# Rotating the last sums through two PSUM banks, and moving transposes and sums within their slots

## The chip, the cores and the metric

One core of a Trainium2 chip. The metric is the time of one execution in device microseconds (us), lower is better. PE is TensorE, PEld its weight loads, DVE is VectorE, ACT is ScalarE, POOL is GpSimd, SP is SyncE, which here issues nearly all transfers. PSUM is the memory that PE writes its sums to, and a bank is one block of it.

## The reference

A retention layer (a recurrence with decay per head) feeds a mixing layer. Shapes: batch 4, 8 heads, sequence 768, head size 64, so 512 channels.

```python
for t in range(S):
    state = gamma * state + einsum('bhd,bhe->bhde', k[:, :, t], v[:, :, t])
    x[:, :, t] = scale * einsum('bhd,bhde->bhe', q[:, :, t], state)
# x as (batch, seq, 512)
theta = x @ w_theta
zr, zi = x * cos(theta), x * sin(theta)
y = w_tok_r @ zr + w_tok_i @ zi          # along the sequence
u = x + y
out = u + relu(u @ w_ch)
```

## The kernel before

The sequence of each batch is cut into three groups of 256 rows, so there are twelve groups n = 0 to 11 for the first half (flip k and q, the masked products, theta, z), and 24 tiles m = 0 to 23 of 128 rows for the second. A loop slot n works on group n, finishes group n - 1, and carries one tile of the second half in slots 3 to 6 and two in slots 7 to 12. The order of the program is the order on each engine.

One tile of the second half is 12 products into y, an addition on DVE that gives u, a transpose of u, four products o, and an output on DVE:

```python
def moe_M(m, lo, hi):                     # y sum, 2 products for each of 6 s0
    b, t0 = divmod(m, nT)
    if lo == 0:
        mo[m] = dict(y=psum.tile([P, dm], FT, name="y_ps", tag="y", bufs=1))
    y_ps = mo[m]["y"]
    ...
def moe_u(m):
    ...
    nc.vector.tensor_add(u, mo[m]["y"], xs[b][:, t0, :])
```

PE may not start the next tile's sum in a bank before DVE has read the last one out of it. The end of the kernel, tiles 18 to 22:

```python
for m in range(last_m - nT + 1, last_m):
    moe_U_dma(m - 1)                      # transpose of u by DMA
    moe_M(m, 0, 4)
    ...
    moe_O(m - 2); moe_out(m - 2); store(m - 2)
    moe_M(m, 4, nT)
    moe_u(m)
moe_last(last_m)
```

The place before the loop:

```python
moe_M(0, 5, nT)
prep(3, "q", DP)        # q scaled, half on DVE, half on POOL
moe_u(0)
prep(3, "v", PP)        # on POOL
w_cast(3)               # on POOL
moe_M(1, 0, 4)          # overwrites the y bank: waits for u of tile 0
flip(3, "q")
moe_M(1, 4, nT)
moe_u(1)
```

The first loop slot, n = 3, puts on POOL: the scaling of q and v of group 4, the casts of w row 4, the cast of wch (the weights of o).

## Time and profile before

| | kernel before |
|---|---|
| median before the prediction | 180.67 us, three runs, 179.34 to 180.89 |
| the profiled run | 179.78 us, span 178.1, mean granted clock 0.998 |
| busy, share of the span | PE 90%, PEld 50%, DVE 57%, ACT 46%, POOL 36% |
| chain that ended last | PE 78%, DMA 6%, DVE 5%, ACT 4%, issue 3%, POOL 3% |

PE is what ends last, so the other engines matter only where PE waits for them.

### The profile page before, as it was taken

How to read it: one execution, taken by the hardware profiler on the slowest of the kernel's cores; microseconds unless marked ns; L12 is line 12 of the kernel's file. 1: busy time of each engine (PE TensorE's matmuls, PEld its weight loads, DVE VectorE, ACT ScalarE, POOL GpSimd, SP SyncE). 2: the span in 40 equal slices, each digit the busy share in tenths (PEclk: the TensorE clock that was granted, in tenths of full speed). 3: DMA queues.
4: the chain of work that ended last, by engine and by line, in shares of the span. 5: the costliest groups of instructions: out<-in, count | busy, mean ns of one | idle time of the engine just before them, and what ended most of it. 6: DMA issues, size and time to landing. Idle time of an engine off the chain costs nothing.

```text
span 178.1 us, 4704 instructions
## 1 busy us (share of the span) xinstructions
PE 161.1 (90%) x1979; PEld 89.5 (50%) x1979; DVE 102.4 (57%) x139; ACT 82.6 (46%) x141; POOL 63.5 (36%) x81
## 2 busy tenths in 40 slices
PE   7889898959889999989999999999999898888892
PEld 2455565624646757555654655545555343333371
DVE  2266698795726777777572983827646154333333
ACT  7236494832456768585738727183471700000000
POOL 5284656490999675914544370000000000000000
PEclk9999999999999999999999999999999999999999
DMA  5999999999999999599999977949163524533343
GB/s 147 312 327 330 288 301 337 339 349 281 337 272 308 291 333 307 137 219 284 223 302 211 292 117 175 162 95 193 30 184 55 156 51 147 95 94 93 94 128 121
DMA packets 66789, 37.92 MB, mean 213 GB/s; under 512 B 24144, under 2 KB 61264, under 8 KB 66768
## 3 DMA queue, kind: packets, MB, share of 16 engines
q1 hardware_dynamic: 66624, 37.50, 82.4%
q8 instruction: 15, 0.25, 0.6%
q10 hardware_dynamic: 144, 0.13, 0.2%
q14 instruction: 6, 0.05, 0.1%
HBM read 25.69 MB, written 6.29 MB: 180 GB/s over the span
## 4 chain that ended last, share of the span: by engine, by line
PE 78%; DMA 6%; DVE 5%; ACT 4%; issue 3%; POOL 3%; DVEq 0%; POOLq 0%
PE y_ps L324 32%; PE o_ps L352 11%; PE th_ps L302 11%; DMA pair<-in_q_dram 6%; PE at_ps L204 4%; PE yT_ps L227 3%; PE y_ps L443 3%; PE kq_ps L183 3%; PE yT_ps L241 3%; PE st_ps L258 3%; DVE u L331 2%; POOL kqb L175 2%; PE y_ps L398 2%; DVE at L211 1%; PE w_ps L378 1%
## 5 line engine op out<-in xcount | busy, mean ns | idle before, releaser
L324 PE MATMUL y_ps<-z,wtr 128*128 128x512 bf16 x138 | 52.4, 379 | 6.2 <-DVE u L331 5.8
L324 PE MATMUL y_ps<-z,wti 128*128 128x512 bf16 x138 | 52.3, 379 | 0.0
L331 DVE TENSOR_TENSOR u<-y_ps,x_sb 128x512 bf16<-128x512 f32 x23 | 15.9, 691 | 32.8 <-PE y_ps L324 32.8
L175 POOL TENSOR_TENSOR kqb<-pair,qscp 128x512 bf16<-128x512 f32 x20 | 22.1, 1123 | 34.8 <-DMA pair<-in_q_dram 32.7
L211 DVE TENSOR_TENSOR at<-at_ps,maskp 128x1024 bf16<-128x1024 f32 x24 | 29.2, 1219 | 2.8 <-PE at_ps L204 2.8
L281 ACT CAST xT<-yT_ps 128x512 bf16<-128x512 f32 x22 | 15.0, 739 | 28.3 <-PE yT_ps L227 28.3
L175 POOL TENSOR_TENSOR kqb<-pair,vscp 128x512 bf16<-128x512 f32 x24 | 25.6, 1085 | 3.0 <-DMA pair<-in_v_dram 2.6
L359 DVE SCALAR_TENSOR_TENSOR ot<-o_ps,u 128x512 f32<-128x512 f32 x23 | 15.9, 690 | 16.5 <-PE o_ps L352 16.3
L324 PEld LDWEIGHTS <-wti 128*128 128x128 bf16 x138 | 13.5, 98 | 20.8 <-issue 8.0
L302 PE MATMUL th_ps<-wth,xT 128*128 128x512 bf16 x96 | 23.5, 379 | 0.1
L352 PE MATMUL o_ps<-wch,uT 128*128 128x512 bf16 x92 | 22.6, 379 | 0.0
L324 PEld LDWEIGHTS <-wtr 128*128 128x128 bf16 x138 | 13.4, 97 | 14.2
L305 ACT ACTIVATE cs<-th_ps,halfpi 128x512 bf16<-128x512 f32 x24 | 16.5, 689 | 8.3 <-PE th_ps L302 7.9
L272 ACT CAST stbd<-st_ps 64x256 bf16<-64x256 f32 x40 | 14.7, 367 | 10.8 <-PE st_ps L258 10.2
L312 DVE TENSOR_TENSOR z<-cs,x_sb 128x1024 bf16<-128x1024 bf16 x24 | 19.0, 829 | 0.0
L186 DVE COPY kqT<-kq_ps 128x1024 bf16<-128x1024 bf16 x17 | 11.5, 687 | 12.0 <-PE kq_ps L183 11.9
L306 ACT ACTIVATE cs<-th_ps,zerob 128x512 bf16<-128x512 f32 x24 | 16.5, 688 | 0.0
L169 ACT CAST kqb<-pair 128x1024 bf16<-128x1024 f32 x12 | 12.6, 1048 | 6.8 <-DMA pair<-in_k_dram 6.8
L410 ACT COPY uT<-u_ps 128x256 bf16<-128x256 bf16 x2 | 0.7, 372 | 31.2 <-PE u_ps L409 31.2
L352 PEld LDWEIGHTS <-uT 128*128 128x128 bf16 x92 | 9.0, 98 | 10.4
L302 PEld LDWEIGHTS <-xT 128*128 128x128 bf16 x96 | 8.9, 98 | 9.9 <-ACT xT L281 0.6
L443 PE MATMUL y_ps<-warm 128*128 128x512 bf16 x31 | 10.9, 478 | 1.3 <-DVE warm L115 1.3
(57 smaller groups left out, 162.8 us busy)
## 6 DMA issues: line engine op xcount, KB each, us to landing
pair<-in_k_dram SPq DMA_DIRECT2D x12, 512.0 KB, 6.8
pair<-in_q_dram SPq DMA_DIRECT2D x12, 512.0 KB, 7.8
pair<-in_v_dram SPq DMA_DIRECT2D x12, 512.0 KB, 8.3
out_dram<-ot SPq DMA_DIRECT2D x23, 256.0 KB, 2.3
wtok<-in_moe_w_tok_r_dram SPq DMA_DIRECT2D x6, 384.0 KB, 6.9
wtok<-in_moe_w_tok_i_dram SPq DMA_DIRECT2D x6, 384.0 KB, 6.4
w<-in_moe_w_theta_dram SPq DMA_DIRECT2D x1, 1024.0 KB, 8.0
w<-in_moe_w_ch_dram SPq DMA_DIRECT2D x1, 1024.0 KB, 9.1
```

The costliest lines, as they stand in the source:

```text
L175: engines[two].tensor_mul(dst[:, two], src[:, two], _bcast_last(sc[:, 2 * g + two], D))
L211: nc.vector.tensor_mul(at.rearrange("p a j t -> p (a j) t"), at_ps.rearrange("p a j t -> p (a j) t"), _bcast_mid(maskp[:, two].rearrange(" ...
L281: copy(st[n, "xT"][:, a].rearrange("e j (i w) -> e j w i", w=2), st[n, "y"][a].rearrange("e j (w i) -> e j w i", w=2))
L302: nc.tensor.matmul(th_ps, st[n, "xT"][:, a, j, :], wth[:, j, :], start=(j == 0), stop=(j == NP - 1))
L305: nc.scalar.activation(cs[:, 0, :], th_ps, AF.Sin, bias=halfpi, scale=1.0)
L306: nc.scalar.activation(cs[:, 1, :], th_ps, AF.Sin, bias=zerob, scale=1.0)
L312: nc.vector.tensor_mul(zs[b][:, c], st[n, "cs", a], _bcast_mid(xs[b][:, c, :], 2))
L324: nc.tensor.matmul(y_ps, wT[r][:, s0, t0 * P:(t0 + 1) * P], zs[b][:, s0, r, :], start=(s0 == 0 and r == 0), stop=(s0 == nT - 1 and r == 1))
L331: nc.vector.tensor_add(u, mo[m]["y"], xs[b][:, t0, :])
L352: nc.tensor.matmul(o_ps, mo[m]["uT"][:, j, :], wch[:, j, :], start=(j == 0), stop=(j == nD - 1))
L359: nc.vector.scalar_tensor_tensor(ot, mo[m]["o"], 0.0, mo[m]["u"], ALU.max, ALU.add)
L443: nc.tensor.matmul(warm_ps, warm[:, 0:P], warm, start=True, stop=True)
```

## The change

Its intent: let the sums of the last tiles alternate between two banks, so that PE need not wait for DVE between tiles; and put work that PE can already do into the holes of the early slots. No work is added or removed.

```diff
     def moe_M(m, lo, hi):
         if lo == 0:
-            mo[m] = dict(y=psum.tile([P, dm], FT, name="y_ps", tag="y", bufs=1))
+            if m < (B - 1) * nT - 1:
+                y_ps = psum.tile([P, dm], FT, name="y_ps", tag="y", bufs=1)
+            else:
+                y_ps = psum.tile([P, dm], FT, name="y_ps", tag="acc", bufs=2)
+            mo[m] = dict(y=y_ps)
 ...
     moe_M(0, 5, nT)
+    moe_u(0)
     prep(3, "q", DP)
-    moe_u(0)
 ...
     moe_u(1)
+    w_tok(3)
     prep(4, "k", K)
 ...  (in the loop)
-        if n == nG:
-            w_tok(3)
 ...
+        if not two and n + 1 >= K_DMA:
+            moe_M(first, 2, 4)
 ...
+        if not two:
+            if n + 1 < K_DMA:
+                moe_M(first, 2, 4)
+            if n in (nG, nG + 1):
+                w_tok(n - nG + 4)
+            moe_M(first, 4, nT)
+            moe_u(first)
+        elif n in pairs:
             moe_M(mine[1], 0, nT)
 ...
         for t in done:
             moe_O(t)
             moe_out(t)
+        if n not in pairs:
+            moe_M(mine[1], 0, nT)
+            moe_u(mine[1])
```

In this code `first` is the slot's first tile (`mine[0]` in the old code), `two` is true in slots with two tiles, nG is 3, `pairs` are the twelve groups (so `n not in pairs` means slot 12), and K_DMA is 7, the first group whose k is flipped by a transfer and not by PE. Smaller lines of the diff (renames, lines that only move) are cut at the marks.

So there are four parts: the end (banks, and the order of slot 12), u of tile 0 ahead of q's scaling, the transposes of w row 3 one slot earlier, and the split of the y sums in slots 3 to 6.

More of the change, by code (lines that the diff above doesn't have):

```diff
@@ L595 @@
             load(n + 3, "q")
-        part = 3 if two else 2
-        moe_M(mine[0], 0, part)
+        first = mine[0]
+        moe_M(first, 0, 3 if two else 2)
         if late:
@@ L603 @@
         if two:
-            moe_M(mine[0], part, nT)
-            moe_u(mine[0])
-        if n == nG:
-            w_tok(3)
-        for name, first in (("k", K_DMA), ("q", Q_DMA)):
-            if nxt and n + 1 < first:
+            moe_M(first, 3, nT)
+            moe_u(first)
+        for name, limit in (("k", K_DMA), ("q", Q_DMA)):
+            if nxt and n + 1 < limit:
                 flip(n + 1, name)
+        if not two and n + 1 >= K_DMA:
+            moe_M(first, 2, 4)
         if nxt and n + 1 >= Q_DMA:
@@ L617 @@
         if n + 1 >= U_DMA:
-            moe_U_dma(mine[0])
+            moe_U_dma(first)
         if n in pairs:
@@ L628 @@
             moe_U(done)
-        if n in (nG, nG + 1):
-            w_tok(n - nG + 4)
-        if two:
+        if not two:
[4 more added lines that the diff above has]
+            moe_M(first, 4, nT)
+            moe_u(first)
+        elif n in pairs:
             moe_M(mine[1], 0, nT)
-        else:
-            moe_M(mine[0], part, nT)
-            moe_u(mine[0])
         if n + 2 in pairs:
@@ L640 @@
             zmul(n - 1, 1)
-        if two:
+        if two and n in pairs:
             moe_u(mine[1])
```

## The prediction

> **What bounds the kernel now.** I read the page first: the span is 178.1 us, TensorE (PE) is busy 90% of it at a granted clock of 0.9 or more throughout, and the chain that ended last is PE work for 78%. So only time in which PE stands still can be gained, and the question is where it stands still. The table by stretches puts it in four places: 33.7 to 54.0 us (16.32 us busy of 20.30), 73.4 to 81.9 (7.95 of 8.50), 137 to 169, and the tail. From 81.9 to 137.0 PE has no gap (55.10 of 55.10).
>
> The waits, longest first, name the releasers. Of all that PE itself waits for, this leads (us in total, times, longest):
>
> ```profile
> PE y_ps L324 <- DVE u L331: 5.8, 7, 1.5
> PE w_ps L378 <- POOL wrow L371: 1.3, 2, 1.0
> PE yT_ps L227 <- ACT cs L306: 1.0, 2, 0.6
> ```
>
> The chain in order of time (start, us, what) shows the first of them as a pattern at the end of the kernel:
>
> ```profile
> 150.69 0.70 DVE u L331
> 151.44 1.89 PE y_ps L324 x8
> 153.33 0.86 PE o_ps L352 x4
> 154.19 0.88 PE y_ps L324 x4
> 155.09 0.70 DVE u L331
> 155.84 1.89 PE y_ps L324 x8
> ```
>
> One tile is 12 products for y and 4 for o, then PE stops until VectorE (DVE) has added x to y, since y has one bank and the next tile's first product overwrites it. The timeline of PE gives the true cost of one such stop:
>
> ```profile
> 150.06 0.38 PE L324 MATMUL y_ps<-z,wtr 128*128 128x512 bf16 x1
> 150.28 0.38 PE L324 MATMUL y_ps<-z,wti 128*128 128x512 bf16 x1
> 151.44 0.38 PE L324 MATMUL y_ps<-z,wtr 128*128 128x512 bf16 x1 [0.78 <-DVE u L331]
> ```
>
> Starts are 0.216 us apart when nothing waits (0.22 here), but 1.16 us across the boundary: 0.944 us lost, more than the 0.78 listed, because the modelled 0.38 of a matmul overlaps its follower. The period is 155.84 - 151.44 = 4.40 us for 16 products, whose issue takes 16 x 0.216 = 3.456.
>
> **What the Trainium skill says.** "Perfetto Trace Analysis", section "Matmuls", wants independent matmul groups to rotate through different PSUM banks so that the evacuation of one overlaps the next group's products. The trace agrees by the opposite: with one bank all 0.944 us are exposed. "PSUM — Partial Sum Buffer", "The four PSUM rules", gives 8 banks of 2 KiB and one output per bank. By the kernel's tiles (tr 2, at 2 because it has 1024 fp32 per partition, acc 2, st 1, y 1) all eight are taken, so a second y bank must be borrowed; the change borrows acc, which is only possible once the y^T and theta sums are finished. "TensorE: Matmul & The Clock Gate", "Back-to-back issue gap", gives N/2.4 + 2.5 ns, so 215.8 ns for N = 512; the trace agrees with 216 ns (that section's other figure, 131 ns sustained, is not what this trace shows). "Perfetto Trace Analysis", "GPSIMD Engine Instruction", calls GpSimd spans unreliable; one term below rests on such a span, and is small.
>
> **The change part by part.** It adds and removes no work: the same matmuls, copies and transfers in another order, and other banks.
>
> *Two banks for tiles 17 to 22, and for 23 against 22.* Stops on u now stand before the y sums of tiles 17, 19, 20, 21, 22 and 23 (chain: 141.98, 150.69, 155.09, 159.49, 163.88, 168.28). Before 18 there is none, as two o groups lie between. The first goes in another way too: in the last slot, the o groups of tiles 14 and 15 move ahead of tile 17's sum. Six times 0.944 = 5.66 us. Next, what could take the place of the wait, with the period at 3.46 us:
> - the acc banks: theta's second sum is last read by ScalarE (ACT) at 142.25, the first at 141.1; tile 17 would start near 141.8 + 1.73 = 143.5 and tile 18 at 146.1. No wait.
> - uT for o(m-2): sum m-2 ends, 0.2 us to the start of u, 0.69 for u, 2.4 to 2.5 from issue to landing, 3.4 to 3.5 in all; o(m-2) comes one period and 8 products later, 3.46 + 1.73 = 5.2. Slack 1.7.
> - the DMA queue: a transpose issue 1.20 and a store 0.34 per period, of 3.46. DVE: 0.69 + 0.69.
> - the tail, where it is closest. Let T be the end of tile 22's issue (now 168.08, from 167.86 + 0.216). The transpose is issued at T + 0.92 and lands at about T + 3.3. Today the last tile's first product starts at 169.02 and o(22) at 172.62, 3.60 later; with that first product at T, o(22) comes at T + 3.60. Slack 0.3: just enough.
>
> ```profile
> 168.28 0.69 DVE L331 TENSOR_TENSOR u<-y_ps,x_sb 128x512 bf16<-128x512 f32 x1 [0.17 <-PE y_ps L324]
> 169.00 1.20 SPq L336 DMA_TRANSPOSE uT<-u  x1
> DMA to landing us min/median/max: 2.4/2.4/2.5
> ```
>
> *The early part, around 38 to 54 us.* u of tile 0 moves ahead of q's scaling (0.92 us) on DVE, so tile 1's sum starts at about 39.0 instead of 39.69; and w transposes of row 3 fill PE in the slot before. But this stretch of the chain does not run through them:
>
> ```profile
> 33.76 10.69 DMA pair<-in_q_dram
> 44.58 1.60 POOL kqb L175 x2
> 46.17 0.41 issue
> ```
>
> The q of group 4 lands at 44.45 whatever PE does; GpSimd (POOL) then scales q and v, casts w row 4 (48.57 to 50.16) and wch (50.10 to 51.99) without a gap. PE cannot flip q before 46.6. So these two moves gain nothing at the end: 0.7 us is won and waited away. After it, four products of tile 2 (0.86 us) now go into the hole of 1.00 in which PE waits for w row 4, and come off the time after it: o(0) could begin at 51.42 rather than 52.29. But it needs wch, ready at about 52.0 to 52.05. Gain 0.24, not 0.86.
>
> *Group 4's slot, 54 to 64 us.* PE waits 0.34 us for ACT to free the transpose bank:
>
> ```profile
> 61.36 0.49 PE L378 MATMUL w_ps<-ident,wrow 128*128 128x128 bf16 x6 [0.34 <-ACT uT L345]
> ```
>
> Four products of tile 3 now lie between. By starts, six transposes of 0.056 take 0.34, and the second six would start at 60.86 but start at 61.36; ACT must only be done at 61.3, when the moved products end. Gain about 0.4. In group 5's slot the moved products end up adjacent to the rest: 0.
>
> *Group 6's slot.* y^T waits for theta's banks until ACT has taken both sine passes of both tiles:
>
> ```profile
> 77.95 0.22 PE L227 MATMUL yT_ps<-at,kqb 64*64 64x128 bf16 x2
> 78.72 0.41 PE L227 MATMUL yT_ps<-at,kqb 64*64 64x128 bf16 x14 [0.55 <-ACT cs L306]
> ```
>
> From 77.95 to 78.72 is 0.77, less about 0.03 for two issues: 0.74 lost. Four products of tile 5 (0.86) now go in front, so y^T arrives after ACT is done. Gain 0.74. DVE and the bank of y follow without a wait, as the order of groups after it is unchanged.
>
> From 81.9 to 137 everything shifts with PE: POOL runs far ahead (q of group 9 is scaled by 84.9 and flipped at 98.2), so no transfer stops PE if it comes 1.4 us earlier.
>
> Sum: 0.24 + 0.4 + 0.74 + 5.66 = 7.0 us. From the median of 180.67: 173.7; I say 173.8, for a small remainder of new waits.
>
> **The rivals.**
> 1. *The transposes of u take the wait's place.* For: one queue issues transposes and stores in order, a transpose's largest time to landing in the whole trace is 6.0 us, and the tail has 0.3 of slack. Against: the last two land in 2.4 to 2.5, and from 147 us the 16 DMA engines are busy only 0.40 of the time. If each period were bound at 4.0 instead of 3.46, 6 x 0.5 = 3 us would go: 176.7.
> 2. *Only the end gains.* The early part stays tied to the loads, or earlier PE work shifts them so that later waits eat the 1.4 us: 180.67 - 5.7 = 175.0. For: the 10.69 us of one q transfer on the chain. Against: no gap of PE from 81.9 to 137.
> 3. *The early gain counts in full.* If wch is ready earlier than POOL's rough span says, 0.86 instead of 0.24: 173.1.
> 4. *Moved work delays ACT.* The evacuation of w row 3 (0.80) now comes ahead of k's cast of group 4 on ACT; flip of k would be near 44.7, still before q's at 46.6. Nothing lost unless q lands earlier.
>
> **Range and chances.** The end's 5.66 is six measured repeats with a clear cause, and slack of 1.7 us in five of them; the early 1.4 is less certain. The three runs before scatter from 179.34 to 180.89, and that noise stays. So 172.6 to 175.4. Faster by over 2% means under 177.06: only rival 1 in a stronger form, or a fault in the order of waits, fails it. 0.95 faster, 0.04 same, 0.01 slower.
>
> **What would show it.** In the changed profile: the wait of y on u falls from 5.8 us in 7 to under 1; the chain at the end has periods of 3.46, with no DVE u in it; the last product of tile 22 and the first of tile 23 start 0.22 apart; o(22) starts 3.6 after that, with at most a small wait for the DMA. Near 52 us o(0) should wait for POOL's wch; near 78 us the wait for cs should be gone; q of group 4 should still land at about 44.4. I am wrong if the periods at the end stay above 3.6, if PE gets new gaps for uT, or if the start of group 7's slot (now 81.9) does not come 1.1 to 1.7 us earlier.

## More of the kernel before

Row 2 of the page cuts the span into 40 slices and gives busy tenths. Of the kernel before:

```profile
PE   7889898959889999989999999999999898888892
PEclk9999999999999999999999999999999999999999
```

PE falls to 5 in one slice (slice 9, near 38 us) and runs at 8 in the last slices. PEclk is the granted clock in tenths of full speed. It shows 9 everywhere in this run.

## The result

| | before | after |
|---|---|---|
| median, four runs each | 180.78 us (179.34 to 181.04) | 171.68 us (171.51 to 172.12) |
| profiled run, span | 178.1 us | 170.4 us |
| its mean granted clock | 0.998 | 1.0 |
| PE busy | 161.1 us (90%) | 158.9 us (93%) |

The ratio is 0.9517, with a 95% interval of 0.9471 to 0.9562. A ratio here is the mean time of one kernel's fast runs over the mean of the other's fast runs of the same rounds, so it is not quite the ratio of the two medians. The direction was right, and 171.68 lies below the predicted range of 172.6 to 175.4.

The chain in order of time at the end of the changed kernel (start, us, what) has no DVE in it any more. From it:

```profile
149.44 0.86 PE o_ps L356 x4
150.30 2.59 PE y_ps L328 x12
152.89 0.86 PE o_ps L356 x4
153.75 2.59 PE y_ps L328 x12
156.34 0.86 PE o_ps L356 x4
```

From 149.44 to 152.89 is 3.45 us per tile, where it was 4.40. Of PE's waits, those that the argument is about are now (us in total, times, longest; the list has eight other entries, of up to 1.3 us):

```profile
PE y_ps L328 <- DVE u L335: 0.8, 1, 0.8
PE yT_ps L227 <- ACT cs L306: 0.5, 1, 0.5
PE o_ps L356 <- POOL wch L582: 0.5, 1, 0.5
PE w_ps L382 <- POOL wrow L375: 0.3, 1, 0.3
```

The first wait fell from 5.8 us in seven to 0.8 in one (the one before tile 1), and the foreseen wait for wch is there.

The landing of the load of q of group 4 and POOL's start on it, in the changed kernel (the same lines of the kernel before are in the prediction):

```profile
33.74 10.18 DMA pair<-in_q_dram
44.06 1.36 POOL kqb L175 x2
```

Where did the 7.7 us between the two spans come from? I compared the starts of the same instructions in both traces:

| stretch | before | after | shorter by | predicted |
|---|---|---|---|---|
| start to POOL's scaling of q of group 4 | 44.58 | 44.06 | 0.52 | 0 |
| from there to the first o | 7.71 | 7.47 | 0.24 | 0.24 |
| to o of tile 2 | 11.13 | 10.63 | 0.50 | 0.4 |
| to o of tile 5 | 17.60 | 16.85 | 0.75 | 0.74 |
| to the end | 97.08 | 91.39 | 5.69 | 5.66 |

Spans are printed to 0.1 us, so the last row, and every figure below that is worked out from a span, carries a rounding of up to 0.1 us; by the first products of tile 23 (169.02 and 161.36) it is 5.65. The four terms of the sum come to 7.18 us, where I had 7.04. So the mechanism and its sizes stand, and yet the times differ by 8.7 us in the means (0.9517 times the before runs' mean of 180.49 is 171.8). About 1.5 us comes from something that the sum does not hold: 0.52 of it is the landing of a load that both kernels issue at 33.7, before the first moved instruction (u of tile 0, at 38), and the rest, about 1.0, is not in these two traces at all. That is what the experiments are for.

Three theories. **Theory 1, landing scatter:** the load of q of group 4 lands at a different time in each run, and everything after it shifts with it. **Theory 2, coupling:** the change makes the early part 2 us faster in a way that I did not see. **Theory 3, the clock**, came with the first runs: in some runs of the kernel before, PE's clock is halved for a while (called a dip below; most such runs are within 1.5% of the fastest of their kernel, so they count as fast runs in the ratios).

### The profile page after: what moved, and what is told of

The parts are those of the page before. It is cut to its first block, busy times and chain, and to the rows that moved or that the text cites. A ratio compares the mean times of both kernels' runs of the same rounds, so it can differ in the third digit from the quotient of the medians.

```text
span 170.4 us, 4701 instructions
## 1 busy us (share of the span) xinstructions
PE 158.9 (93%) x1979; PEld 88.5 (52%) x1979; DVE 101.3 (59%) x139; ACT 82.7 (49%) x141; POOL 62.4 (37%) x81
## 4 chain that ended last, share of the span: by engine, by line
PE 77%; DMA 8%; DVE 3%; POOL 3%; ACT 3%; issue 2%; DVEq 0%; POOLq 0%
PE y_ps L328 32%; PE th_ps L302 12%; PE o_ps L356 12%; DMA pair<-in_q_dram 6%; PE at_ps L204 4%; PE kq_ps L183 3%; PE yT_ps L227 3%; PE yT_ps L241 3%; PE st_ps L258 3%; DMA pair<-in_k_dram 2%; PE y_ps L402 2%; DVE at L211 1%; POOL kqb L175 1%; ACT kqb L169 1%; PE w_ps L382 1%
## 5 line engine op out<-in xcount | busy, mean ns | idle before, releaser
L175 POOL TENSOR_TENSOR kqb<-pair,qscp 128x512 bf16<-128x512 f32 x20 | 21.1, 1073 | 33.1 <-DMA pair<-in_q_dram 27.9
L312 DVE TENSOR_TENSOR z<-cs,x_sb 128x1024 bf16<-128x1024 bf16 x24 | 17.4, 763 | 0.4 <-DMA x_sb<-xT 0.4
L183 PE MATMUL kq_ps<-ident,kqb 128*128 128x128 bf16 x136 | 10.1, 219 | 2.9 <-DVE kqb L175 1.0
```

What stands on the lines that cost most here:

```text
L175: engines[two].tensor_mul(dst[:, two], src[:, two], _bcast_last(sc[:, 2 * g + two], D))
L183: nc.tensor.transpose(ps[:, two, j, :], st[n, name][:, two, j * P:(j + 1) * P], ident)
L312: nc.vector.tensor_mul(zs[b][:, c], st[n, "cs", a], _bcast_mid(xs[b][:, c, :], 2))
```

## The experiments

Each kernel had five rounds (six runs) beside the kernel before on the same chip. The three batches ran on three chips. Their runs of the kernel before had medians of 180.5, 179.35 and 179.35 us, 11 runs each.

### Batch 1: repeats, and the two halves of the change

**before_again.** No edit.

> The kernel before against itself, for the noise and a second profile of it. Theory 1 (scatter): every term of my sum was right (0.25 + 0.49 + 0.74 + 5.66 = 7.14 us in the two profiles), and the 2 us beyond it come from when the load of q of group 4 lands, which differs from run to run whatever the kernel; then this run's times spread over 1 to 2 us, and in its profile a shift of that landing shows as the same shift of everything after it. Theory 2 (coupling): the change itself makes the early part faster by 2 us more than I summed; then the time here is steady near 180.8 and the landing is near 44.4 again. Ratio 0.995 to 1.005 in both.

Measured: median 180.07 us (179.03 to 180.85), ratio 0.9972 [0.9922, 1.0022]. The surprise is in its profiled run, of 180.85 us. The slices of the page:

```profile
PE   7789898949889999989999999999999988788892
PEclk9999999996999999999999999999999999999999
```

One slice of PEclk is 6. The timeline of PE in that trace (start, us, engine, line, operation, tiles, and in brackets the idle time before it) shows why:

```profile
37.26 0.38 PE L324 MATMUL y_ps<-z,wti 128*128 128x512 bf16 x1
39.83 0.45 PE L324 MATMUL y_ps<-z,wtr 128*128 128x512 bf16 x1 [2.19 <-DVE u L331]
40.07 0.63 PE L324 MATMUL y_ps<-z,wti 128*128 128x512 bf16 x1
40.50 0.63 PE L324 MATMUL y_ps<-z,wtr 128*128 128x512 bf16 x1
40.92 0.63 PE L324 MATMUL y_ps<-z,wti 128*128 128x512 bf16 x1
```

After a stop of 2.19 us before tile 1 the same product takes 0.63 us instead of 0.38, and starts come 0.43 apart instead of 0.216: half speed. The table by stretches gives 0.50 as the clock from 40.0 to 43.4 (last three columns: clock, DMA share, GB/s), and 1.64 us of PE busy in the 4.0 us before, against 2.08 in the profile that I predicted from, which kept its clock.

```profile
40.00:43.40 3.40, 3.18 (x11) 1.38 (x11) 0.00 (x0) 1.04 (x1) 0.00 (x0) 0.50 1.17 295
```

The chain of this run goes through DVE's scaling of q and u of tile 0, not through the load of q of group 4:

```profile
37.87 1.30 DVE kqb L175
39.17 0.61 DVE u L331
39.79 0.04 issue
39.83 3.01 PE y_ps L324 x7
```

In the first profile q's scaling took 0.92 us, here 1.32 by the timeline; in both POOL was casting w row 3 for most of that time, and why it took longer is not shown. It is also not what made the stop longer: u of tile 0 ended at about the same time in both (tile 1 starts at 39.69 and 39.83), but tile 0's last product came at 37.26 here and at 37.85 there. The trace that I had predicted from was of a run without a dip.

**after_again.** No edit.

> The changed kernel again, five rounds, second profile. Theory 1: with more rounds the ratio comes up from 0.9517 towards 1 - 7.14/180.7 = 0.9605. Theory 2: it stays at 0.951 to 0.953.

Measured: median 172.67 us (171.46 to 175.62), ratio 0.9555 [0.951, 0.960] without the slow run, between the two theories. This points to an effect nearer to 4.5% than to 4.8%, though the interval still holds both. The profiled run was the slow one, 175.62 us at a mean clock of 0.979: q of group 4 started on POOL only at 45.77, PE stood longer (waits of 1.15 and 0.96 us between 43.8 and 46.9), and the clock was halved from about 47.1 to 53.9. Being a slow run, it is used for no comparison; it shows only that the changed kernel is not immune.

**end_only.** The kernel before with the end of the change alone:

```diff
-            mo[m] = dict(y=psum.tile([P, dm], FT, name="y_ps", tag="y", bufs=1))
+            (acc bank from tile 17 on, as in the change)
...
+        if n not in pairs:      # slot 12: o of the done tiles first
+            moe_M(mine[1], 0, nT)
+            moe_u(mine[1])
...
```

> The kernel before with the two banks for tiles 17 to 22 and the new order of the last slot, nothing else. Both theories: 6 x 0.944 = 5.66 us off, so about 175.1 and a ratio of 0.9687; all periods at the end 3.46 us. A rival in which the two banks also change anything earlier would show more than that.

Measured: 174.42 us (173.53 to 175.73), ratio 0.9683 [0.9631, 0.9734], where 0.9687 was expected. Two of the six runs had a dip, the profiled one among them.

**early_only.** The changed kernel with those two edits taken back:

```diff
-            (acc bank from tile 17 on)
+            mo[m] = dict(y=psum.tile([P, dm], FT, name="y_ps", tag="y", bufs=1))
...
-        elif n in pairs:
+        else:
             moe_M(mine[1], 0, nT)
...     (and `if two and n in pairs` is `if two` again)
-        if n not in pairs:
-            moe_M(mine[1], 0, nT)
-            moe_u(mine[1])
```

> The changed kernel with one bank for y and the old order of the last slot, so only the early moves (u of the first tiles, w row 3, the split of the sums in short slots). Theory 1: 0.25 + 0.49 + 0.74 = 1.5 us off, ratio 0.992. Theory 2: 3.4 us off, ratio 0.981, and the group after wch (the first o) starts more than 0.25 us earlier relative to the landing of q of group 4 than in the kernel before.

Measured: 177.95 us (177.35 to 179.28), ratio 0.9876 [0.983, 0.9922], between theory 1 (0.992) and theory 2 (0.981). Its profile decides: span 176.3 with q of group 4 at 44.33, so 131.97 from there to the end, against 133.52 in the first profile of before. That is 1.55 us, the early terms of my sum. Theory 2 falls: relative to the landing nothing else became faster.

### Batch 2: the stop before tile 1, and the wait for wch

**u0_only.** The kernel before with one line moved:

```diff
+    moe_u(0)
     prep(3, "q", DP)
-    moe_u(0)
```

> The kernel before with one line moved: u of tile 0 ahead of q's scaling on DVE. My prediction gave this move nothing at the end. Theory 3 (clock): in 7 of 17 runs of the kernel before the mean granted clock was 0.987 to 0.99 and the time 180.87 us in the mean, against 179.65 in the other ten; in the profile of such a run PE stood 2.19 us before tile 1's sum and then ran at half clock for about 3.5 us. With u moved the stop is shorter: runs at 0.99 become rare (0 or 1 of 6), mean 179.3 to 179.8, ratio 0.994 to 0.998. Theory 1 (landing scatter alone): ratio 1.000 and as many runs at 0.99 as before.

Measured: 179.02 us (178.62 to 179.72), ratio 0.9978 [0.9938, 1.0019], no run of six under a clock of 0.997. From the first chip, where 7 of 17 runs of the kernel before had a low clock, two or three of six would be expected in the old order. But on this chip the kernel before had only two of eleven, so the count alone does not prove it.

**u0_filler.** The old order, with PE kept busy in the stop:

```diff
     moe_u(0)
+    fill_ps = psum.tile([P, dm], FT, name="th_ps", tag="acc", bufs=2)
+    for _ in range(7):
+        nc.tensor.matmul(fill_ps, warm[:, 0:P], warm, start=True, stop=True)
```

> The kernel before in its old order, with seven products of zeros into a free acc bank put where PE waits for u of tile 0 (7 x 0.216 = 1.5 us, inside the wait of 1.46 to 2.19). It removes no wait and adds work. Theory 3 (clock): no run at 0.99 from this spot, mean near 179.6, ratio 0.994 to 0.998, although nothing comes earlier. If instead the order of the work matters and not the clock: 1.000, or slower by some tenths.

Measured: 179.46 us (179.03 to 179.98), ratio 1.0002 [0.9958, 1.0046]; no run under 0.997. The extra work costs nothing at full clock, and the span from q of group 4 on is 133.51, as in the first profile (133.52). It gained nothing in the mean: the ratio is the one expected if the clock did not matter, and a miss for the 0.994 to 0.998 of theory 3. With dips in only two of eleven runs of the kernel before on this chip there was little to gain, so it settles nothing.

**u0_back.** The changed kernel with that line moved back:

```diff
-    moe_u(0)
     prep(3, "q", DP)
+    moe_u(0)
```

> The changed kernel with that one move taken back. Theory 3: runs with the clock at 0.99 are frequent again (2 to 4 of 6) and the mean is 0.5 to 1.0 us above the changed kernel's 172.1, so ratio near 0.960. Theory 1: 172.1 as the changed kernel, ratio 0.9555.

Measured: 171.87 us (171.56 to 172.73), ratio 0.9584 [0.9544, 0.9624]; one run of six with a low clock (0.986), where I had expected two to four. In its profile the stop was 1.24 us, not 2.19, and the span from q of group 4 is 126.36, as in the changed kernel (126.34). A miss for theory 3 in its size: at full clock this move is worth nothing, as predicted.

**wch_early.** The changed kernel, with the cast of wch where POOL idles:

```diff
     w_cast(3)
+    nc.gpsimd.tensor_copy(wch, wdma["ch"])
...
             w_cast(4)
-            nc.gpsimd.tensor_copy(wch, wdma["ch"])
```

> The changed kernel with POOL's cast of wch moved from after w row 4 to before the scaling of q of group 4, where POOL idles 3.5 us waiting for that load. It tests the term where I said o(0) waits for wch (0.46 us of wait in the changed kernel). If so: the wait is gone, o(0) follows the y products, 0.6 us off: mean 171.5, ratio 0.952. If w row 4 or another wait takes over at once, no gain. The load of wch must land by about 41; if it lands later, POOL is held up and it gets slower.

Measured: 171.34 us (170.73 to 171.88), ratio 0.9545 [0.9506, 0.9583]. From q of group 4 on, 125.68 us: 0.66 less than the changed kernel. The first o now follows the y products with no wait. By starts that wait cost 0.62 us in the changed kernel (50.69 to 51.53, less 0.216), which is the gain within the rounding, so the limit of that term (0.24 and not 0.86) was POOL's cast, as predicted.

### Batch 3: the stop doubled, and the remaining parts alone

**u0_late.** The kernel before, with DVE scaling that half of q a second time, into a scratch tile:

```diff
     prep(3, "q", DP)
+    scr = work.tile([P, dm], BF, name="scr", bufs=1)
+    nc.vector.tensor_mul(scr..., raw[3, "q"]..., _bcast_last(qscp[:, 0], D))
     moe_u(0)
```

> The kernel before with DVE scaling the first half of q twice (once into a scratch tile) before u of tile 0, so PE's stop there grows by 0.9 to 1.3 us. Theory 3 (the stop brings the clock down): runs at a mean clock of 0.99 or below in at least 4 of 6, where the kernel before has 9 of 28; the time in those 181 to 182, in runs at full clock 179.3 to 180, since PE still reaches q's flip near the time that POOL has q. If the clock dips have nothing to do with this stop: as many as in the kernel before in the same rounds, and 179.3 to 180.5 in all.

Measured: 182.36 us (181.75 to 182.72), ratio 1.013 [1.0064, 1.0196]; six of six runs with a mean clock of 0.981 to 0.991, where the kernel before in the same rounds had three of eleven. This is the clearest result on the clock: lengthen the stop and every run has a low clock. The timeline of PE of this kernel:

```profile
41.33 0.38 PE L324 MATMUL y_ps<-z,wtr 128*128 128x512 bf16 x1 [3.41 <-DVE u L331]
41.97 0.58 PE L324 MATMUL y_ps<-z,wti 128*128 128x512 bf16 x1
42.34 0.63 PE L324 MATMUL y_ps<-z,wtr 128*128 128x512 bf16 x1
```

The half clock lasts from about 42.0 to 45.4. I had put such runs at 181 to 182; five of the six lie above that. The longer stop itself also delays PE beyond the point where POOL has q ready: in the profile POOL is done with q of group 4 at 45.59, and PE flips it only at 48.98. So the time of this kernel is not the price of the dip alone.

**w3_only.** The kernel before with w_tok(3) moved, nothing else:

```diff
     moe_u(1)
+    w_tok(3)
     prep(4, "k", K)
...
-        if n == nG:
-            w_tok(3)
```

> The kernel before with only the transposes of w row 3 moved to the slot before. Nothing at the end: in the profile the span less the start of POOL's scaling of q of group 4 stays 133.5 us (178.1 - 44.58 in the kernel before; 177.4 - 43.89 and 177.8 - 44.35 in two others that change nothing after it), ratio 0.998 to 1.002.

Measured: 179.74 us (178.76 to 180.51), ratio 0.9983 [0.992, 1.0046]; from q of group 4 on, 133.47 us. Worth nothing, as predicted.

**split_only.** The kernel before with the split of the sums of tiles 2 to 5 alone:

```diff
+        if not two and n + 1 >= K_DMA:
+            moe_M(mine[0], 2, 4)
         if nxt and n + 1 >= Q_DMA:
...
+        if not two and n + 1 < K_DMA:
+            moe_M(mine[0], 2, 4)
         if n in (nG, nG + 1):
             w_tok(n - nG + 4)
...
-            moe_M(mine[0], part, nT)
+            moe_M(mine[0], 4, nT)
```

> The kernel before with only the split of the y sums of tiles 2 to 5 (four products earlier in their slots). My terms 0.25 + 0.49 + 0.74 = 1.5 us are all here: span less POOL's start of q of group 4 about 132.0 (as 176.3 - 44.33 in the kernel with all early moves), ratio 0.992. If the splits need the other two moves to pay, it stays nearer 133.5.

Measured: 177.9 us (177.63 to 178.91), ratio 0.9893 [0.9833, 0.9953]; from q of group 4 on, 131.98 us. All 1.5 us of the early gain at full clock come from the splits.

**q4_shared.** wch_early, and q of group 4 shared between DVE and POOL:

```diff
             ret_mask(n, 0)
+        if n == nG:
+            prep(n + 1, "q", DP)
+            prep(n + 1, "v", PP)
+            w_cast(4)
...     (the same lines are taken out at the start of slot 3)
```

> The changed kernel with wch cast early (gave 0.66 us at equal landing) and, besides, q of group 4 scaled half by DVE (after the first mask) and half by POOL. The law that the end follows POOL's chain from the landing of that q says: POOL is through 1.02 us earlier, so w row 4 and all after it come up to 1.0 us earlier: 170.4, ratio 0.950, span less POOL's start of q about 124.7 against 125.7. If another wait (the transpose bank that ACT frees, DVE's longer queue) takes over, 125.2 to 125.7.

Measured: 171.01 us (170.12 to 172.45), ratio 0.9508 [0.9446, 0.9569]. From q of group 4 on, 125.26 us, 0.42 less than wch_early and 1.08 less than the changed kernel, so by that column this version beats both. The times do not settle it against wch_early: the two ran on different chips, and their intervals overlap. It is not the full 1.0 of the expectation, and POOL's timeline names the wait that took over:

```profile
43.14 1.04 POOL L175 TENSOR_TENSOR kqb<-pair,qscp 128x512 bf16<-128x512 f32 x1 [1.54 <-DMA pair<-in_q_dram]
44.66 2.04 POOL L175 TENSOR_TENSOR kqb<-pair,vscp 128x512 bf16<-128x512 f32 x2 [0.48 <-DMA pair<-in_v_dram]
```

With its share of q done early, POOL now waits 0.48 us for v of the same group, and the chain of this run goes through that load:

```profile
35.67 8.85 DMA pair<-in_v_dram
44.66 0.92 POOL kqb L175
```

From POOL's start on v to the end it is 123.7 us in both kernels (168.4 - 44.66, and 170.1 - 46.42 in wch_early), so nothing after v became faster.

### All profiles on one scale

| kernel | span | POOL starts q of group 4 | from there to the end | mean clock |
|---|---|---|---|---|
| before | 178.1 | 44.58 | 133.52 | 0.998 |
| u0_filler | 177.4 | 43.89 | 133.51 | 1.0 |
| w3_only | 177.8 | 44.33 | 133.47 | 1.0 |
| u0_only | 177.8 | 44.35 | 133.45 | 1.0 |
| before_again | 179.1 | 44.64 | 134.46 | 0.99 |
| split_only | 177.2 | 45.22 | 131.98 | 1.0 |
| early_only | 176.3 | 44.33 | 131.97 | 1.0 |
| end_only | 174.0 | 45.09 | 128.91 | 0.99 |
| after | 170.4 | 44.06 | 126.34 | 1.0 |
| u0_back | 169.9 | 43.54 | 126.36 | 1.0 |
| wch_early | 170.1 | 44.42 | 125.68 | 1.0 |
| q4_shared | 168.4 | 43.14 | 125.26 | 1.0 |
| u0_late (other work added) | 180.5 | 43.55 | 136.95 | 0.991 |
| after_again (slow, not compared) | 173.9 | 45.77 | 128.13 | 0.979 |

Three things vary. What is the same to 0.07 us for kernels that should be equal is the fourth column at full clock. The third column moves from 43.14 to 45.22 us over the fast runs, with no pattern by kernel that I can see, and at full clock the span follows it one for one (theory 1). In the three fast profiles with a dip (before_again, end_only, u0_late) the chain does not go through that load, but through DVE's work before tile 1 and PE at half clock. There the fourth column also depends on how early the load came, so the 0.94 us by which before_again exceeds before is no fixed price of a dip. For the six stops these two runs give, from o of tile 5 to the first product of tile 23, 88.00 us in before_again (82.12 to 170.12) and 82.34 in end_only (82.62 to 164.96), so 5.66.

## Why the prediction was right or wrong

**Right: the six stops.** 5.66 us predicted, 5.65 in the two traces by starts, 5.66 in end_only. No transpose took the wait's place: the period is 3.45 us, and in the tail o of tile 22 starts 3.60 us after the first product of tile 23 (164.96 and 161.36), as worked out, with no idle time before it. Rival 1 did not happen. The second bank was counted rightly, though the count of eight stands in "PSUM — Partial Sum Buffer" under "Specifications (TRN2)", not in the section that the prediction names.

**Right: the early terms at full clock.** 0.24, 0.50 and 0.75 against 0.24, 0.4 and 0.74. That the first o would be held by POOL's cast of wch is confirmed by the wait of 0.5 us and by wch_early. Rivals 2 and 3 are out: the early gain came through to the end, and not more of it. split_only puts all of it down to the splits. Rival 4 went as foreseen: k is flipped at 44.78, ahead of q at 46.16. That the two other moves "gain nothing at the end" held at full clock (u0_only, w3_only and u0_back in the fourth column); whether the first of them also saves dips is open, see below.

**Wrong: the start of the subtraction.** The step that failed is "From the median of 180.67: 173.7", and with it the constant landing and the range. I took 7.0 us, read from a trace of an undisturbed run, off a median of 180.67 us, and called the spread of the three runs noise. The runs show two sources of that spread. First, the clock. Over the 39 runs of the kernel before in the three batches, 12 had a mean clock of 0.991 or below; they took 180.95 us in the mean, the other 27 took 179.44 (two of these 27 took 181.02 and 181.39 at full clock, so a dip is not needed for a long run). That makes 12/39 x 1.51 = 0.46 us in the mean of the kernel before, which I had put at zero because the one profile that I had showed none. The profiled run itself had taken 179.78 us; from there the sum gives 172.7. Second, the landing of q of group 4: my text has it at 44.45 "whatever PE does", which is right as to cause and wrong as a constant. In the profiles POOL starts on it between 43.14 and 45.77 (45.22 without the slow run), and at full clock the end moves with it. A range of 2.8 us around that start was too narrow.

In steps from the predicted 173.8 to the measured 171.68 (2.12 us; the steps add up to it within rounding): 0.89 us is the median against the profiled run (180.67 and 179.78), 0.52 the landing in the two profiles, 0.14 the terms, 0.16 my allowance for new waits and rounding, and 0.44 the changed kernel's own median against its profiled run (171.68 and 172.12). The first and the last are differences between runs, which the traces do not explain.

The means are 179.90 us for before (the same 39 runs) and 172.07 for the changed kernel (nine fast runs), 7.83 us apart: 7.18 from the terms, about 0.46 from the clock if the changed kernel were free of dips, and the remaining 0.2 is put down to landing scatter, which no run isolates. These runs come from more than one chip. The first four runs of each lay on opposite sides of these means, 180.49 and 171.75, by luck as far as the record shows.

**What stays open.** That a longer stop brings the clock down is shown by u0_late (six of six). The other profiles fit: with the old order the stop before tile 1 was 2.19 us in the two that dipped there (before_again, end_only) and 1.24 to 1.46 in the four that did not (before, w3_only, split_only, u0_back); with the new order it was 0.78 to 0.95. What seems to count is how much PE works in a stretch of about 3.4 us, and not one stop: in the 3.41 us before the clock fell PE was busy for 1.22 us in before_again, 1.27 in end_only, 0.69 in u0_late and 1.30 in after_again, whose longest stop there was 1.15, while in the ten profiles that kept their clock the emptiest 3.41 us between 34 and 57 us held 1.49 (in before). That is a pattern in the profiles, not tested by a run of its own. That moving u of tile 0 makes the dips rarer is likely but not settled. In all kernels with the old order there (63 runs) 16 had a mean clock of 0.991 or below, in all with the new order (34 runs) three, and two of those three were of early_only; the three chips differ among themselves, with five, two and three of eleven for the kernel before. So I cannot say how much of the 0.46 us the change really removes. Of the 1.51 us between runs with and without a dip the one pair of profiles shows 0.94; the other half microsecond is not resolved. Why the load lands at different times was not explored, and no run moved the landing alone. The clocks of the first four runs of before are not on record, so whether dips made their median high is only argued.

**My own check list.** Of what I said would show the steps, these held: periods of 3.45, the wait on u under 1 us, 0.21 us from the last product of tile 22 to the first of tile 23 (161.15 and 161.36), the wait for cs in slot 6 gone. Two failed, both by the landing. It was not "at about 44.4": the load landed at 43.92 (33.74 + 10.18). And group 7's slot did not start 1.1 to 1.7 us earlier, but 2.0 (o of tile 5, the last work before it, at 79.01 instead of 81.02), of which 0.52 is the landing. By my own words the second was a sign of being wrong.

## What to carry to other kernels

When a wait between two groups of matmuls repeats, measure it start to start (0.944 us here, not the listed 0.78), count the repeats, and check each resource that could take its place. Such a sum held to about 0.15 us here. Before taking it off a time, find out which state the traced run was in and take it off that run's time, since a median over runs with and without a halved clock is not the same starting point. And look at PE's stops for what they do to the clock afterwards, not only for their own length: a hole that is waited away anyway can still cost when it is long enough to slow the products behind it.

## What the Trainium skill lacked or had wrong

- "TensorE: Matmul & The Clock Gate", section "What's actually happening", says that the clock is halved after an idle window of about 3.4 us, and that the window runs freely. I should have drawn on it. The half rate, its length and the dependence on chance agree: 0.50 from 40.0 to 43.4, and a low mean clock in 12 of 39 runs of one kernel. But a whole idle window, as that section has it, was not needed: the clock fell after a stop of 2.19 us, in a stretch of 4.0 us in which PE was busy for 1.64. (A later section of that page, "A second HAM failure mode: psum-queue depth-cycling", does say that short and frequent idling can do it, without a figure.) In the kernel whose profiled run stood for 3.41 us, six of six runs had a low clock.
- The same page, section "Back-to-back issue gap", gives 131 ns as the sustained spacing for N = 512 in a real kernel. Here it is 216 ns in the uninterrupted streams (twelve y products and the first o after them, from 146.69 to 149.28 in the changed kernel), as its formula for the isolated gap says.
- "Perfetto Trace Analysis", section "GPSIMD Engine Instruction", says to treat a GpSimd span as unreliable. For the one plain cast that could be checked here it held: the cast of wch ended at 49.59 + 1.89 = 51.48, and the product that waited for it started at 51.53.
- None of the pages that I read says how far the landing of one load varies between runs. Here POOL's start on one load was at 44.06 and 45.77 us in two runs of the changed kernel (the second a slow run), and between 43.14 and 45.22 in the fast profiles of all kernels, one for one in the time at full clock.
